# Softmax sums of two heads in one column-tiled block, values of both heads in the next iteration: a 32-head attention loop on one core

## The chip, the cores and the metric

The kernel runs on one core of a Trainium2 chip. The metric is the device time of one execution in microseconds. A ratio below is the mean time of one kernel's fast runs over that of the kernel before in the same rounds, so not quite the ratio of the medians that stand beside it; below 1 is faster. Times of different rounds are compared through the kernel before, which ran in all of them.

## The reference

Four layers in turn, each added to its input: a spectral filter (A), a memory attention (B), A, B. The change concerns B alone (shortened; `...` marks cuts):

```python
# x: (1, 2048, 640) bf16; 64 segments of 32 rows, 8 memory rows before each; 32 heads of 128
for s in range(n_seg):
    h = jnp.concatenate([mem, xs], axis=1)
    q, k, v = (jnp.einsum('btd,dhe->bhte', h, W) for W in (Wq, Wk, Wv))
    scores = jnp.where(mask, jnp.einsum('bhqe,bhke->bhqk', q, k) * scale, -1e9)
    p = _softmax(scores, axis=-1)
    o = jnp.einsum('bhqk,bhke->bhqe', p, v)
    o = jnp.einsum('bhte,hed->btd', o, Wo)
    mem = o[:, :M, :]
    ...
```

The kernel takes all segments at once with a guess for the memory rows, checks the guess, and falls back to a general path if it is off.

## The kernel before

Iteration `h` of the head loop projects K, Q and V of head `h`, computes scores of head `h - 1` (Exp on ScalarE, mask product on VectorE, giving P), sums P of head `h - 1` over the keys, and multiplies P of head `h - 2` with V. The **sums** use a stationary operand of ones with 32 columns. Four of them run side by side in the array, one for each quarter of its columns, writing partitions 0, 32, 64 and 96:

```python
        def sums(h, P, ps_last):
            psl = pa.tile([128, 512], FP32, name="psl", tag="psl", bufs=1)
            jobs = []
            for i in range(max(len(r) for r in runs[:-1])):
                for g_ in range(NG - 1):
                    t, (_, lo, hi, off) = runs[g_][i]
                    b = lo - st.q0[g_] + (PRE if g_ else 0)
                    jobs.append((g_, psl[:, b:b + hi - lo], off, i == 0, i == len(runs[g_]) - 1))
            tail, (_, lo, hi, off) = runs[-1][0][1], runs[-1][1][1]
            top = ps_last[:, 512 - SW:512]
            for g_ in range(NG - 1):
                jobs.append((g_, top, off + SW * g_, True, g_ < NG - 2))
            jobs.append((NG - 2, top[:, SW - (tail[2] - tail[1]):SW], tail[3], False, True))
            for g_, dst, off, first_, last_ in jobs:
                nc.tensor.matmul(dst[32 * g_:32 * g_ + 32, :], lhsT=ones[:, 0:32], rhs=P[:, off:off + dst.shape[1]], start=first_, stop=last_,
                                 skip_group_check=True)
            v, nx = x_view(psl, PRE, GS), GS * SEG
            nc.scalar.copy(out=sums_sb[:, 0:nx].rearrange("p (r s j) -> p r s j", r=16, j=2), in_=byclass(v))
            nc.scalar.copy(out=sums_sb[:, nx:nx + GS], in_=v[:, :, SEG])
            nc.scalar.copy(out=sums_sb[0:32, NR - PRE:NR], in_=psl[0:32, 0:PRE])
            nc.scalar.copy(out=sums_sb[:, NR - PRE - SW:NR - PRE], in_=top)

        def sums_ln(h):
            nc.scalar.activation(out=Rs[h % 2], in_=sums_sb, func=ACTF.Ln, bias=g["floor"][:, 0:1])
            if h:
                nc.gpsimd.tensor_tensor(out=accS, in0=accS, in1=sums_sb, op=ALU.add)
            else:
                nc.gpsimd.tensor_copy(out=accS, in_=sums_sb)
            if 0 < h < H - 1:
                sums_acc(h - 1)

        def sums_acc(h):
            if h:
                nc.gpsimd.tensor_tensor(out=accR, in0=accR, in1=Rs[h % 2], op=ALU.add)
            else:
                nc.gpsimd.tensor_copy(out=accR, in_=Rs[0])

        def sums_back(h):
            R = Rs[h % 2]
            nc.scalar.activation(out=R, in_=R, func=ACTF.Exp, scale=-1.0)
            if h == H - 1:
                return
            Rd = g["dram"].tile([1, 4 * NR], FP32, name="Rd", tag="Rd", bufs=3)
            nc.sync.dma_start(out=Rd[0:1, :].rearrange("o (g n) -> (o g) n", g=4), in_=R[0:128:32, :])
            nc.sync.dma_start(out=Rbs2[h % 2], in_=Rd[0:1, :].to_broadcast([128, 4 * NR]))
```

The reciprocals are a row per quarter; they go to DRAM and come back as a broadcast to all partitions, for VectorE to multiply with when it evicts the value matmuls from PSUM. They are made on ScalarE as Ln of the sums and Exp of the negated Ln. A chain is a row of matmuls that add up in one PSUM bank, for a run of some 500 columns five of them. `merge` deals the dependent work out between the dense units, a projection chain or two each:

```python
        def merge(dense, dep):

            n = 0
            for i, f in enumerate(dense):
                f()
                while n * len(dense) < (i + 1) * len(dep):
                    dep[n]()
                    n += 1

# ... in the loop, for each h:
                dense, parts, groups = [], [], []
                if h < H:
                    def both(run):
                        return [lambda: (run(w, h, NG - 1), run(w, h, 0))] + [lambda g_=g_: run(w, h, g_) for g_ in range(1, NG - 1)]

                    dense += both(k_run)
                    dense += [lambda: q_m(w, h)] if h < 2 else both(q_run)
                    vt = [lambda t=t: v_tiles(w, h // 2, t) for t in range(0, NT, 2)]
                    dense += vt[5:] if h % 2 else vt[:5]
                post = [lambda: None] * 3
                if 1 <= h <= H:
                    P[h - 1] = Ps[(h - 1) % 2]
                    Rb[h - 1] = Rbs2[(h - 1) % 2]
                    parts = [lambda part=part: last_ps.update({h - 1: score_part(h - 1, P[h - 1], part)}) for part in st.parts]
                    post = [lambda: sums(h - 1, P[h - 1], last_ps[h - 1]), lambda: sums_ln(h - 1), lambda: sums_back(h - 1)]
                if h >= 2:
                    oT[h - 2] = oTs[h % 2]
                    groups = [lambda g_=g_: value_group(h - 2, P[h - 2], Rb[h - 2], oT[h - 2], g_) for g_ in range(NG)]
                if h < H:
                    g1 = groups + [lambda: None] * (NG - len(groups))
                    merge(dense, parts + [g1[0], post[0], g1[1], post[1], g1[2], post[2], g1[3], g1[4]])
# ... (cut: iterations 32 and 33, and the output projection)
```

TensorE's PSUM banks: three for projections, two for scores, two for value groups, one for the wide sums. All are in use.

## Time and profile before

| | before |
|---|---|
| time, median of the 4 runs beside the changed kernel | 1572.94 us (1571.74 to 1574.16) |
| span in the profile | 1569.8 us |
| busy: TensorE, VectorE, ScalarE | 98%, 50%, 52% |
| two heads of the loop (even and odd) | 32.40 us |
| column-tiled blocks of sums in the two B layers | 64, of 21 matmuls each |

How to read it: TensorE is the only engine without idle time in the loop, so a pair of heads lasts as long as TensorE's stream of instructions. A matmul's end in the profile is computed (the prediction names the page of the Trainium skill that says so). For what a matmul really takes one goes by its start and the start of the next. "Edge" or "excess" below means the distance between two starts less what the first streams, its columns at 2.4 per ns, the rate that the prediction reads from the trace. The prediction shows the lines.

### The profile page before, as it was taken

The page shows a single profiled execution, that of the slowest core. Times are in us where ns is not written, and L with a number is a line of the kernel's source. Part 1 is how long each engine was busy: PE and PEld are TensorE (multiplying, and loading weights), DVE is VectorE, ACT ScalarE, POOL GpSimd, SP SyncE. Part 2 cuts the span into 40 slices and gives each one's busy share as a digit, 9 for nine tenths or more (in the row PEclk, how much of TensorE's full clock was granted, in tenths as well). Part 3 has the DMA queues.
Part 4 walks back from the last instruction along what each step waited for, and adds up shares of the span by engine and source line. Part 5 has one row for each costly group of instructions (what it writes and reads, how often), then busy time and mean ns, then how long its engine had stood idle before and what let it go on. Part 6 is the DMA issues. An engine that isn't in the chain of part 4 may idle for free. (4 is left out here: it accounts for less than half of the span.)

```text
span 1569.8 us, 36492 instructions
## 1 busy us (share of the span) xinstructions
PE 1536.3 (98%) x14418; PEld 1072.5 (68%) x14419; DVE 787.4 (50%) x2198; ACT 818.5 (52%) x2485; POOL 228.5 (15%) x327
## 2 busy tenths in 40 slices
PE   7999999999999999999999999999999999999998
PEld 5676676666766666677766766666766666677776
DVE  7872555455555545533377535455555545553111
ACT  4484665666666566511126655666666566662000
POOL 3620111111111111100034101111111111110000
PEclk9999999999999999999999999999999999999999
DMA  4680545446454553636114515446454554537242
GB/s 171 210 302 12 151 134 138 137 121 178 123 151 123 136 163 106 218 98 178 51 49 148 189 54 136 138 122 177 124 150 123 136 163 131 143 98 229 68 125 67
DMA packets 159763, 214.78 MB, mean 137 GB/s; under 512 B 7136, under 2 KB 133096, under 8 KB 151648
## 3 DMA queue, kind: packets, MB, share of 16 engines
q1 hardware_dynamic: 159008, 210.08, 45.8%
q8 instruction: 114, 1.87, 0.5%
q0 software_dynamic: 576, 2.30, 0.4%
q14 instruction: 65, 0.53, 0.1%
HBM read 167.26 MB, written 45.10 MB: 135 GB/s over the span
## 5 line engine op out<-in xcount | busy, mean ns | idle before, releaser
L1086 PEld LDWEIGHTS <-bB_S 128*128 128x128 bf16 x3180 | 258.2, 97 | 174.3 <-issue 0.9
L1245 DVE TENSOR_TENSOR bB_S<-pso,bB_S 128x480 bf16<-128x480 f32 (+1 forms) x320 | 194.2, 607 | 237.3 <-PE pso L1231 226.5
L1165 ACT ACTIVATE bB_S<-pss 128x269 bf16<-128x269 f32 (+5 forms) x576 | 204.2, 387 | 196.4 <-PE pss L1162 191.3
L1399 PE MATMUL psx<-Wo_sb,bB_S 128*128 128x320 bf16 x2048 | 287.7, 299 | 0.1
L1145 DVE CAST bB_S<-psk 128x495 bf16<-128x495 f32 (+3 forms) x320 | 191.7, 600 | 112.6 <-PE psk L1086 82.8
L1399 PEld LDWEIGHTS <-bB_S 128*128 128x128 bf16 x2048 | 197.1, 98 | 74.4 <-DVE bB_S L1245 0.7
L1166 DVE TENSOR_TENSOR bB_S<-bB_S,maskf 128x269 bf16<-128x269 bf16 (+5 forms) x576 | 158.3, 289 | 162.0 <-ACT bB_S L1165 162.0
L1154 ACT CAST bB_S<-psv 128x512 bf16<-128x512 f32 (+1 forms) x288 | 161.4, 560 | 86.5 <-PE psv L1152 83.3
L1130 ACT ACTIVATE bB_S<-psq 128x96 bf16<-128x96 f32 x300 | 152.7, 509 | 91.6 <-PE psq L1086 90.7
L1196 POOL TENSOR_TENSOR bB_S<-bB_S,bB_S 128x535 f32<-128x535 f32 x62 | 69.9, 1128 | 726.8 <-ACT bB_S L1191 713.9
L1152 PE MATMUL psv<-bB_S,B1hT_S 128*128 128x256 bf16 x1360 | 166.2, 273 | 0.0
L1152 PE MATMUL psv<-bB_S,B2hT_S 128*128 128x256 bf16 x1360 | 166.2, 273 | 0.0
L1086 PE MATMUL psk<-B1hT_S,bB_S 128*128 128x495 bf16 (+3 forms) x800 | 162.3, 343 | 0.3 <-ACT bB_S L1107 0.2
L1086 PE MATMUL psk<-B2hT_S,bB_S 128*128 128x495 bf16 (+3 forms) x800 | 162.3, 343 | 0.2 <-ACT bB_S L1107 0.2
L1162 PEld LDWEIGHTS <-bB_S 128*128 128x128 bf16 x1152 | 98.4, 98 | 84.4
L1086 PE MATMUL psq<-B1hT_S,bB_S 128*128 128x495 bf16 (+5 forms) x780 | 153.2, 336 | 0.0
L1086 PE MATMUL psq<-B2hT_S,bB_S 128*128 128x495 bf16 (+5 forms) x780 | 153.2, 336 | 0.0
L1152 PEld LDWEIGHTS <-B2hT_S 128*128 128x128 bf16 x1360 | 127.5, 98 | 13.3 <-issue 0.2
L1152 PEld LDWEIGHTS <-B1hT_S 128*128 128x128 bf16 x1360 | 127.5, 98 | 13.3 <-issue 0.2
L1162 PE MATMUL pss<-bB_S 128*128 128x132 bf16 (+8 forms) x1152 | 132.0, 219 | 0.1
L1231 PE MATMUL pso<-bB_S,bB_S 128*128 128x132 bf16 (+8 forms) x1152 | 118.9, 219 | 1.7 <-DVE oTmf L1248 1.2
L1231 PEld LDWEIGHTS <-bB_S 128*128 128x128 bf16 x1152 | 89.4, 98 | 20.5 <-DVE oTmf L1246 2.2
(281 smaller groups left out, 1472.8 us busy)
## 6 DMA issues: line engine op xcount, KB each, us to landing
bB_S<-Rd SPq DMA_DIRECT2D x62, 1070.0 KB
oTx_d<-bB_S SPq DMA_DIRECT2D x60, 512.0 KB
bB_S<-oTx_d SPq DMA_DIRECT2D x46, 512.0 KB
bB_S<-in_B_Wq_dram SPq DMA_DIRECT2D x32, 320.0 KB
bB_S<-in_B_Wk_dram SPq DMA_DIRECT2D x32, 320.0 KB
bB_S<-in_B_Wv_dram SPq DMA_DIRECT2D x32, 320.0 KB
Wo_sb<-in_B_Wo_dram SPq DMA_DIRECT2D x4, 1280.0 KB
B1wv_S<-in_B_Wv_dram SPq DMA_DIRECT2D x10, 512.0 KB
```

The lines of the kernel that those rows point to most:

```text
L1086: nc.tensor.matmul(ps, lhsT=w[:, ch, hh * 128:(hh + 1) * 128], rhs=src[:, ch, lo:hi], start=(ch == 0), stop=(ch == 4))
L1130: nc.scalar.mul(out=qv[:, :, 0:SEG], in_=x_view(ps, o, n)[:, :, 1:SW], mul=scale)
L1145: nc.vector.tensor_copy(out=KTs[h % 2][:, lo:hi], in_=ps[:, 0:hi - lo])
L1152: nc.tensor.matmul(ps[:, i * 256:(i + 1) * 256], lhsT=hT[:, ch, st.hcol((t + i) * 128):st.hcol((t + i) * 128) + 128], rhs=w["Wv"][:, ch, : ...
L1154: nc.scalar.copy(out=V[:, t:t + n, :].rearrange("p a b -> p (a b)"), in_=ps[:, 0:n * 256])
L1162: nc.tensor.matmul(ps[:, off - o0:off - o0 + hi - lo], lhsT=KT[:, t * 128:(t + 1) * 128], rhs=QT[:, lo:hi], start=True, stop=True)
L1165: nc.scalar.activation(out=E[:, 0:n], in_=ps[:, 0:n], func=ACTF.Exp)
L1166: nc.vector.tensor_tensor(out=P[:, o0:o0 + n], in0=E[:, 0:n], in1=bs.mask[:, o0:o0 + n], op=ALU.mult)
L1196: nc.gpsimd.tensor_tensor(out=accS, in0=accS, in1=sums_sb, op=ALU.add)
L1231: nc.tensor.matmul(pso[:, lo - q0:hi - q0], lhsT=V[:, t, (h % 2) * 128:(h % 2 + 1) * 128], rhs=P[:, off:off + hi - lo], start=(i == 0), st ...
L1245: nc.vector.tensor_tensor(out=oT.rearrange("p (r s j) -> p r s j", r=16, j=2)[:, :, s0:s0 + ns, :], in0=byclass(po), in1=rx, op=ALU.mult)
L1399: self.tc.nc.tensor.matmul(ps[:, 0:320], lhsT=lhs(h, k // 2), rhs=self.g["Wo_sb"][:, h, c0:c0 + 320], start=(h == 0), stop=(h == H - 1))
```

## The change

Its intent is to halve how often TensorE goes into the column-tiled mode and out of it. In even iterations one block holds the sums of two heads; the value matmuls of both wait for the following odd iteration, because only then are the reciprocals there. For pairs the copies of the sums from PSUM move from ScalarE to VectorE. The core of the diff:

```diff
-        def sums(h, P, ps_last):
-            psl = pa.tile([128, 512], FP32, name="psl", tag="psl", bufs=1)
-            jobs = []
-            for i in range(max(len(r) for r in runs[:-1])):
+        def sums(heads, ps_last):
+            jobs, outs = [], []
+            for n, h in enumerate(heads):
+                psl = pa.tile([128, 512], FP32, name="psl", tag="pso" if n else "psl", bufs=2 if n else 1)
+                top = ps_last[:, 512 - SW * (n + 1):512 - SW * n]
+                outs.append((sums_sb[h % 2], psl, top))
+                for i in range(max(len(r) for r in runs[:-1])):
+                    for g_ in range(NG - 1):
+                        t, (_, lo, hi, off) = runs[g_][i]
+                        b = lo - st.q0[g_] + (PRE if g_ else 0)
+                        jobs.append((h, g_, psl[:, b:b + hi - lo], off, i == 0, i == len(runs[g_]) - 1))
+            tail, (_, lo, hi, off) = runs[-1][0][1], runs[-1][1][1]
+            for n, h in enumerate(heads):
+                top = outs[n][2]
                 for g_ in range(NG - 1):
-                    t, (_, lo, hi, off) = runs[g_][i]
-                    b = lo - st.q0[g_] + (PRE if g_ else 0)
-                    jobs.append((g_, psl[:, b:b + hi - lo], off, i == 0, i == len(runs[g_]) - 1))
-            tail, (_, lo, hi, off) = runs[-1][0][1], runs[-1][1][1]
-            top = ps_last[:, 512 - SW:512]
-            for g_ in range(NG - 1):
-                jobs.append((g_, top, off + SW * g_, True, g_ < NG - 2))
-            jobs.append((NG - 2, top[:, SW - (tail[2] - tail[1]):SW], tail[3], False, True))
-            for g_, dst, off, first_, last_ in jobs:
-                nc.tensor.matmul(dst[32 * g_:32 * g_ + 32, :], lhsT=ones[:, 0:32], rhs=P[:, off:off + dst.shape[1]], start=first_, stop=last_,
+                    jobs.append((h, g_, top[:, :], off + SW * g_, n == 0, g_ < NG - 2))
+                jobs.append((h, NG - 2, top[:, SW - (tail[2] - tail[1]):SW], tail[3], False, True))
+            for h, g_, dst, off, first_, last_ in jobs:
+                nc.tensor.matmul(dst[32 * g_:32 * g_ + 32, :], lhsT=ones[:, 0:32], rhs=P[h][:, off:off + dst.shape[1]], start=first_, stop=last_,
                                  skip_group_check=True)
-            v, nx = x_view(psl, PRE, GS), GS * SEG
-            nc.scalar.copy(out=sums_sb[:, 0:nx].rearrange("p (r s j) -> p r s j", r=16, j=2), in_=byclass(v))
-            nc.scalar.copy(out=sums_sb[:, nx:nx + GS], in_=v[:, :, SEG])
-            nc.scalar.copy(out=sums_sb[0:32, NR - PRE:NR], in_=psl[0:32, 0:PRE])
-            nc.scalar.copy(out=sums_sb[:, NR - PRE - SW:NR - PRE], in_=top)
+            copy = nc.vector.tensor_copy if len(heads) == 2 else nc.scalar.copy
+            for sb, psl, top in outs:
+                v, nx = x_view(psl, PRE, GS), GS * SEG
+                copy(out=sb[:, 0:nx].rearrange("p (r s j) -> p r s j", r=16, j=2), in_=byclass(v))
+                copy(out=sb[:, nx:nx + GS], in_=v[:, :, SEG])
+                copy(out=sb[0:32, NR - PRE:NR], in_=psl[0:32, 0:PRE])
+                copy(out=sb[:, NR - PRE - SW:NR - PRE], in_=top)
 ...
-            Rd = g["dram"].tile([1, 4 * NR], FP32, name="Rd", tag="Rd", bufs=3)
-            nc.sync.dma_start(out=Rd[0:1, :].rearrange("o (g n) -> (o g) n", g=4), in_=R[0:128:32, :])
-            nc.sync.dma_start(out=Rbs2[h % 2], in_=Rd[0:1, :].to_broadcast([128, 4 * NR]))
+            Rd[h] = g["dram"].tile([1, 4 * NR], FP32, name="Rd", tag="Rd", bufs=4)
+            nc.sync.dma_start(out=Rd[h][0:1, :].rearrange("o (g n) -> (o g) n", g=4), in_=R[0:128:32, :])
+            if h % 2 or h == H - 2:
+                for a in range(h if h == H - 2 else h - 1, h + 1):
+                    nc.sync.dma_start(out=Rbs2[a % 2], in_=Rd[a][0:1, :].to_broadcast([128, 4 * NR]))
 ...
-                dense, parts, groups = [], [], []
+                dense, parts = [], []
                 if h < H:
                     def both(run):
                         return [lambda: (run(w, h, NG - 1), run(w, h, 0))] + [lambda g_=g_: run(w, h, g_) for g_ in range(1, NG - 1)]
 
-                    dense += both(k_run)
-                    dense += [lambda: q_m(w, h)] if h < 2 else both(q_run)
+                    ks, qs = both(k_run), [lambda: q_m(w, h)] if h < 2 else both(q_run)
                     vt = [lambda t=t: v_tiles(w, h // 2, t) for t in range(0, NT, 2)]
-                    dense += vt[5:] if h % 2 else vt[:5]
-                post = [lambda: None] * 3
+                    vt = vt[5:] if h % 2 else vt[:5]
+                    for n in range(5):
+                        dense += (ks[n:n + 1] if h % 2 else []) + qs[n:n + 1] + vt[n:n + 1]
+                    if h % 2 == 0:
+                        dense = ks + dense
+                pause = lambda: None
                 if 1 <= h <= H:
                     P[h - 1] = Ps[(h - 1) % 2]
                     Rb[h - 1] = Rbs2[(h - 1) % 2]
                     parts = [lambda part=part: last_ps.update({h - 1: score_part(h - 1, P[h - 1], part)}) for part in st.parts]
-                    post = [lambda: sums(h - 1, P[h - 1], last_ps[h - 1]), lambda: sums_ln(h - 1), lambda: sums_back(h - 1)]
-                if h >= 2:
-                    oT[h - 2] = oTs[h % 2]
-                    groups = [lambda g_=g_: value_group(h - 2, P[h - 2], Rb[h - 2], oT[h - 2], g_) for g_ in range(NG)]
+
+                def values(a):
+                    oT[a] = oTs[a % 2]
+                    return [lambda g_=g_: value_group(a, P[a], Rb[a], oT[a], g_) for g_ in range(NG)]
+
+                def post_of(*heads):
+                    return [lambda: sums(heads, last_ps[heads[-1]])] + [f for a in heads for f in (lambda a=a: sums_ln(a), lambda a=a: sums_back(a))]
+
                 if h < H:
-                    g1 = groups + [lambda: None] * (NG - len(groups))
-                    merge(dense, parts + [g1[0], post[0], g1[1], post[1], g1[2], post[2], g1[3], g1[4]])
+                    if h % 2 == 0:
+                        dep = parts + ([pause] + post_of(h - 2, h - 1) + [pause] * 11 if h else [])
+                    elif h == 1:
+                        dep = parts
+                    else:
+                        v0, v1 = values(h - 3), values(h - 2)
+                        v0[4] = lambda f=v0[4]: (f(), store(h - 3, oT[h - 3]))
+                        v1[4] = lambda f=v1[4]: (f(), store(h - 2, oT[h - 2]))
+                        if h < H - 1:
+                            dep = [pause, pause, v0[0]]
+                            for f, p in zip(v0[1:] + v1, parts):
+                                dep += [p, f]
+                        else:
+                            dep = [pause]
+                            for f, p in zip(v0, parts):
+                                dep += [f, p]
+                            dep += parts[5:] + [pause]
+                            for f, p in zip(post_of(h - 1), v1):
+                                dep += [f, p]
+                            dep += v1[3:]
```

Cut: two buffers for the sums in place of one, the accumulators for the range check, and iterations 32 and 33, which do the same as before.

## The prediction

> **What bounds the kernel now.** I read the page first, its busy row and its chain, then the chain of waits, then windows and the timeline inside the head loop of layer B, and last the timeline of the DMA queue. The page gives
>
> ```profile
> PE 1536.3 (98%) x14418; PEld 1072.5 (68%) x14419; DVE 787.4 (50%) x2198; ACT 818.5 (52%) x2485; POOL 228.5 (15%) x327
> PE 43%; DMA 0%; DVE 0%; ACT 0%; SPq 0%; issue 0%; DVEq 0%
> ```
>
> TensorE is busy for 98% of the span, VectorE and ScalarE for half of it, and of the chain that ended last every step that carries a share is TensorE's. Two heads of the loop, cut at the first K matmul of each, in windows:
>
> ```profile
> 430.36:462.75 32.39, 32.39 (x302) 21.96 (x301) 16.98 (x50) 20.41 (x65) 4.50 (x5) 1.00 0.47 132
> 445.74:462.75 17.01, 17.01 (x160) 11.71 (x159) 8.78 (x27) 10.40 (x33) 2.58 (x3) 1.00 0.56 155
> 462.75:478.14 15.39, 15.39 (x146) 10.26 (x145) 8.20 (x24) 10.02 (x32) 1.93 (x3) 1.00 0.37 107
> ```
>
> The columns are window, its length, busy us of PE, PEld, DVE, ACT and POOL, granted clock, DMA share and rate. The even head takes 17.01 us, the odd one 15.39 (it has four value-projection units where the even has five), PE without a gap in both, at the full clock. So a pair costs 32.40 us, and only TensorE's own instruction stream can shorten it; work that goes from ScalarE to VectorE buys nothing here by itself.
>
> A busy PE may still lose time between matmuls. I took the start of every matmul in the trace and subtracted from the distance to the next one the streaming time of the first, columns divided by 2.4 per ns (five matmuls of 499 columns start 1.05 us apart in all, below, which is that rate and 2 to 3 ns each). For the dense matmuls between 200 and 690 us the rest is 2 to 3 ns. It is large in two places only, at the two edges of the column-tiled softmax sums:
>
> ```profile
> 449.66 1.22 PE L1086 MATMUL psk<-B1hT_S,bB_S 128*128 128x499 bf16 x5
> 450.71 0.40 PE L1162 MATMUL pss<-bB_S 128*128 128x132 bf16 x4
> ...
> 439.58 1.22 PE L1086 MATMUL psq<-B1hT_S,bB_S 128*128 128x499 bf16 x5
> 440.73 0.42 PE L1185 MATMUL psl<-bB_S,ones 128*32 128x139 bf16 x16
> 440.98 0.20 PE L1185 MATMUL pss<-bB_S,ones 128*32 128x33 bf16 x5
> 441.12 0.41 PE L1231 MATMUL pso<-bB_S,bB_S 128*128 128x132 bf16 x4
> ```
>
> These are timeline rows: start, time, engine and line, tiles, count. Before an ordinary matmul the chain of five takes 450.71 - 449.66 = 1.05 us; before the block it takes 440.73 - 439.58 = 1.15 us, so **going in costs 0.10 us**. The block's 16 wide sums start over 0.25 us, 16 ns apart, a quarter of what one of some 132 columns streams (55 ns), so four column groups do run at once. The five narrow ones (33 or 5 columns) have 0.14 us to the next ordinary matmul, though they need some 0.05, so **coming out costs 0.09 us**. Over the 27 blocks between 200 and 690 us the medians are 97 ns in and 96 ns out; with the usual 3 ns taken off, 94 + 93 = 0.187 us a block. The chain of waits also holds
>
> ```profile
> PEld L1185 <- issue: 25.4, 62, 0.4
> ```
>
> which is not 0.41 us lost per block: it is the weight loader's idle time, most of it beside the matmuls of the Q chain. Only matmul starts count.
>
> **What the Trainium skill says.** "TensorEngine Tiling (Array Packing)", Key Properties, says that changing the tiling mode, unlike changing the tile, drains TensorE. It gives no figure; the trace agrees and gives 0.187 us for both ways. "TensorE: Matmul & The Clock Gate", section Back-to-back issue gap, has columns / 2.4 + 2.5 ns for a warm matmul; the trace has 2 to 3 ns over the streaming time. "Perfetto Trace Analysis", section Tensor Engine Instruction, says that a matmul's end in the profile is computed, not observed; hence I count from starts, and the 98% alone proves nothing.
>
> **The change part by part.**
> 1. *Fewer blocks.* In the built order of instructions I counted runs of 32-column matmuls: 64 runs of 21 before; after, 30 of 42 (one per pair, heads 0 to 29 of each of the two layers) and 4 of 21 (heads 30 and 31). The sum is 1344 both times, and TensorE has as many instructions as before. Thirty switches in and out go: 30 x 0.187 = **5.6 us**. Inside a block nothing changes; four groups are fed in the same rotation, and 42 take twice what 21 do.
> 2. *Sum copies go from ScalarE to VectorE* for pairs: 4 x 60 instructions. On ScalarE they take 0.58 + 0.22 + 0.17 + 0.21 = 1.18 us a head; VectorE's eviction of the same 480 columns takes 0.66, so some 1.2 us. ScalarE loses about 71 us in all, VectorE gains about 72. Neither is on the path: 0.
> 3. *Value matmuls of two heads in odd iterations.* TensorE's total is the same. From the pieces (K and Q 4.5 us each, a head's scores 1.0, its values 1.0, value projection 5.5 even and 3.8 odd, sums 0.3 a head) I estimate for the even iteration 4.5 + 4.5 + 5.5 + 1.0 + 0.6 + 0.2 = 16.3 us, and for the odd 4.5 + 4.5 + 3.8 + 1.0 + 2.0 = 15.8. VectorE in the odd one has five K casts of 0.60 (3.0 us), nine mask products of 0.29 (2.6) and the value evictions of two heads (5 x 0.61, and six small ones of 0.16: 4.0 a head): some 13.6 us of duration in 15.8, 86%. Consecutive VectorE rows overlap by about 0.1 us in the timeline, so the real load is lower. Busy, not the bound: 0.
> 4. *Broadcast of the reciprocals.* Today a write of the row and a broadcast per head, each iteration; after, both writes, then both broadcasts. No bytes more, but two broadcasts stand one behind the other. See the second rival.
> 5. *Ends.* Heads 30 and 31 and the output projection keep their order; the chain after the loop is unmoved: 0.
>
> Sum: 1574.06 - 5.6 = **1568.5 us**. A pair would take 32.40 - 0.19 = 32.21 us.
>
> **The rivals.**
> *A: VectorE or ScalarE holds PSUM back.* VectorE is strictly in order, and in the odd iteration value evictions, mask products (which wait for ScalarE's Exp) and K casts queue behind each other. Value groups come about 0.9 per projection unit, so two banks for them cover some 3 us, and an eviction ends some 2 us after its matmuls when a mask product ahead of it is late. The projection's three banks cover three units, also some 3 us. In the even iteration Ln, Exp, Ln, Exp (0.74 and 0.66) stand between Q and V evictions, and the first Ln waits for VectorE's copies; ScalarE should run about 1.5 us late for three units, still inside three banks. For it: both margins are about 1 us. Against it: PE waits for almost nothing in the loop today. If it comes, I would expect 0.2 to 0.5 us a pair, 6 to 15 us in all: 1569 to 1578.
>
> *B: the broadcast lands late.* Today:
>
> ```profile
> 461.61 0.50 SPq L1214 DMA_DIRECT2D Rd<-R  x1
> 463.36 0.34 SPq L1215 DMA_DIRECT2D bB_S<-Rd  x1
> ...
> 464.00:467.00 3.00, 3.00 (x23) 1.68 (x21) 2.27 (x6) 1.22 (x4) 0.00 (x0) 1.00 0.82 137
> 467.00:471.00 4.00, 4.00 (x30) 2.28 (x29) 2.21 (x7) 2.69 (x12) 0.00 (x0) 1.00 0.80 302
> ```
>
> The broadcast leaves 1.75 us after the row's write and moves 1.07 MB at 137 GB/s, later 302: 0.41 MB by 467 us, the rest 2.2 us later, so it lands about 5.9 us after its issue (estimate). Afterwards, from the end of the sums: copies and Ln to 1.9 us, second Exp at about 4.6, first broadcast issued at 5.2, landed at about 11.1. The first value group's matmuls end at about 10.4 (seven units of 1.05 to 1.1 in the even iteration, two of 1.3 in the odd one). VectorE would wait 0.7 us, and PE needs that bank again only at about 13.1. So I expect the wait to show on VectorE and to cost nothing; if the pair's two broadcasts slow each other by 2 us or more, PE stalls and up to 1 us a pair returns, 1569 to 1595 at worst. The second broadcast, needed some 7 us later, has room.
>
> *C: the idle time of the weight loader was a real loss of 0.41 us.* Then 30 x 0.41 = 12.3 us go, to about 1562. The starts of the matmuls speak against it.
>
> **Range and chances.** The gain has a ceiling near 5.6 us, since nothing else in the loop waits; the three runs of before spread over 2.3 us. Stalls of A or B might eat part or a little more than all. I take 1565.5 to 1574.5. A gain of 2% would need 31 us, over five times the switches removed: 0.01. A loss of 2% needs a stall of 1 us in every pair: 0.01. Within 2%: 0.98.
>
> **What would show it.** Right: 34 blocks, about 0.10 us into and 0.09 out of each, a pair period of 32.2 us, VectorE busy near 860 us and ScalarE near 748, no PE row in the chain of waits worth over a few us. B: an idle row of VectorE's value eviction released by the broadcast, and gaps at the third value group. A: gaps before value or projection matmuls in odd iterations, released by VectorE or ScalarE. The prediction is wrong if the pair period stays at 32.4 with the blocks halved, or falls well below 32.1, which would mean that a switch costs more than its edges show.

## The result, and the profile after

| | before | after |
|---|---|---|
| median, 4 runs each, same rounds | 1572.94 us | 1566.86 us (1565.62 to 1568.15) |
| ratio, 95% interval | | 0.9961, 0.9944 to 0.9979 |
| span in the profile | 1569.8 us | 1563.9 us |
| pair of heads | 32.40 us | 32.20 us |

The change is worth 6.1 us of the median, and 5.5 us in a second set of rounds (1572.76 less 1567.27, below): within 2%, but clear of the noise. The page after, its busy row and the chain that ended last:

```profile
PE 1529.1 (98%) x14418; PEld 1072.3 (69%) x14419; DVE 816.3 (52%) x2438; ACT 768.7 (49%) x2245; POOL 238.6 (15%) x329
PE 41%; DMA 1%; ACT 0%; DVE 0%; issue 0%; SPq 0%; DVEq 0%; ACTq 0%
```

TensorE has the same number of instructions, 14418 matmuls, and is 7.2 us less busy; ScalarE has 240 instructions fewer and VectorE 240 more, the 4 x 60 copies. In the windows of a pair, cut at the first K matmul of each head (columns as in the prediction):

```profile
443.12:475.32 32.20, 32.20 (x302) 22.01 (x301) 17.93 (x59) 18.75 (x58) 4.87 (x4) 1.00 0.39 134
443.12:459.39 16.27, 16.27 (x163) 10.99 (x162) 7.41 (x27) 10.73 (x32) 4.87 (x4) 1.00 0.41 118
459.39:475.32 15.93, 15.93 (x141) 11.01 (x139) 10.53 (x32) 8.01 (x26) 0.00 (x0) 1.00 0.37 150
```

Both halves are still full of TensorE work, and the pair is 0.20 us shorter than the 32.40 of before. VectorE now has 10.53 us in the odd half, ScalarE 10.73 in the even. The block itself, in TensorE's timeline (start, us, engine and line, tiles, count):

```profile
450.00 1.25 PE L1153 MATMUL psv<-bB_S,B1hT_S 128*128 128x256 bf16 x10
451.18 0.67 PE L1190 MATMUL psl<-bB_S,ones 128*32 128x139 bf16 x32
451.67 0.26 PE L1190 MATMUL pss<-bB_S,ones 128*32 128x33 bf16 x10
451.86 1.22 PE L1087 MATMUL psq<-B1hT_S,bB_S 128*128 128x495 bf16 x5
```

From the V chain's first matmul to the block are 1.18 us, where its ten matmuls need 10 x (256 / 2.4 + 2.5 ns) = 1.09; the edge in is there once, and once more on the way out. Over all blocks of the trace, one of 42 lasts 0.769 us with both edges, one of 21 lasted 0.481. Two of 21 against one of 42 is 2 x 0.481 - 0.769 = 0.193 us of the 0.20 that a pair gains. Of the rows that are new in the list of waits, this one bears on rival B:

```profile
DVE bB_S L1250 <- DMA bB_S<-Rd: 57.6, 31, 4.7
```

VectorE's value evictions wait for the broadcast of the reciprocals, 1.8 us a pair on average ((57.6 - 4.7) / 30; the wait of 4.7 us stands at the end of the second layer). Before, they had waited for TensorE in all but 2 of 237 us. That wait and what it costs are the subject of one experiment.

### The profile page after: what moved, and what is told of

It reads as the page before. It is cut to its first block, busy times and chain, and to the rows that moved or that the text cites. A ratio compares the mean times of both kernels' runs of the same rounds, so it can differ in the third digit from the quotient of the medians.

```text
span 1563.9 us, 36413 instructions
## 1 busy us (share of the span) xinstructions
PE 1529.1 (98%) x14418; PEld 1072.3 (69%) x14419; DVE 816.3 (52%) x2438; ACT 768.7 (49%) x2245; POOL 238.6 (15%) x329
## 5 line engine op out<-in xcount | busy, mean ns | idle before, releaser
L1166 ACT ACTIVATE bB_S<-pss 128x269 bf16<-128x269 f32 (+5 forms) x576 | 208.9, 386 | 138.6 <-PE pss L1163 138.3
L1206 POOL TENSOR_TENSOR bB_S<-bB_S,bB_S 128x535 f32<-128x535 f32 x90 | 111.6, 1253 | 820.0 <-DVE bB_S L1198 762.2
L1250 DVE TENSOR_TENSOR bB_S<-pso,bB_S 128x480 bf16<-128x480 f32 (+1 forms) x320 | 192.6, 602 | 75.1 <-DMA bB_S<-Rd 57.6
L1163 PE MATMUL pss<-bB_S 128*128 128x132 bf16 (+8 forms) x1152 | 137.6, 219 | 0.0
```

Source lines behind the costliest of these rows:

```text
L1163: nc.tensor.matmul(ps[:, off - o0:off - o0 + hi - lo], lhsT=KT[:, t * 128:(t + 1) * 128], rhs=QT[:, lo:hi], start=True, stop=True)
L1166: nc.scalar.activation(out=E[:, 0:n], in_=ps[:, 0:n], func=ACTF.Exp)
L1206: nc.gpsimd.tensor_tensor(out=acc, in0=acc, in1=part, op=ALU.add)
L1250: nc.vector.tensor_tensor(out=oT.rearrange("p (r s j) -> p r s j", r=16, j=2)[:, :, s0:s0 + ns, :], in0=byclass(po), in1=rx, op=ALU.mult)
```

## The experiments

The theory: **what is saved is the way into and out of the column-tiled mode, 0.19 us each time**. Rivals: the new order of values and projections, or ScalarE's relief, made the gain; or an extra weight load is what costs. All kernels gave correct results.

### Sums of the two heads in two blocks again

Everything else of the change stays. The first attempt:

```diff
-dep = parts + ([pause] + post_of(h - 2, h - 1) + [pause] * 11 if h else [])
+dep = parts + ([lambda: sums((h - 2,), last_ps[h - 1], 0, True),
+               lambda: sums((h - 1,), last_ps[h - 1], 1, True)]
+              + post_of(h - 2, h - 1)[1:] + [pause] * 11 if h else [])
```

with `sums` taking the place `n` of a lone head, and copies on VectorE.

> The changed kernel, but the two heads' softmax sums stand in two column-tiled blocks of 21 matmuls with one projection unit between them, in place of one block of 42; value matmuls, copies on VectorE, order of Ln, Exp and broadcasts stay. Theory (the gain is the switching in and out of the column-tiled mode): 64 blocks again, a pair period of 32.20 + 0.19 = 32.39 us, the whole about 30 x 0.19 = 5.7 us slower than the changed kernel, so equal to the kernel before within 1 us (ratio 0.999 to 1.001). Rival (the gain is from the new order of value matmuls and of the projections, or from ScalarE's relief): the pair period stays at 32.20 and the time at about 1567 us.

Measured: 1594.25 us, ratio 1.0138 (1.0121 to 1.0154), a pair of 33.15 us. That fits neither theory. The chain of waits, TensorE's rows, names what happened:

```profile
PE pss L1190 <- ACT bB_S L1166: 16.9, 30, 0.6
```

The narrow sums (into pss) of the first block use the bank of the last scores. In this edit they follow those scores without a projection unit between them, and TensorE waits for ScalarE's Exp to have read the bank: 30 times, with an excess of 0.73 us between the matmul starts. The edit had brought in a wait of its own. Less that wait the pair would be 33.15 - 0.73 = 32.42 us, near the 32.39 of the theory, but that is a subtraction and no test. Mended: the lone first block puts its narrow sums into a value bank, which is idle in even iterations.

```diff
 top = ps_last[:, 512 - SW * (n + 1):512 - SW * n]
+if alone and n == 0:
+    top = pa.tile([128, 512], FP32, name="pso", tag="pso")[:, 0:SW]
 ...
-jobs.append((h, g_, top[:, :], off + SW * g_, n == 0, g_ < NG - 2))
+jobs.append((h, g_, top[:, :], off + SW * g_, n == 0 or alone, g_ < NG - 2))
```

> The split into two blocks of 21 again, mended. In the first split run the pair period was 33.15 us, of which 0.73 us was one wait that the edit itself had brought in: the narrow sums of the first block go into the bank of the last scores and now followed them directly, so they waited for ScalarE's Exp of those scores. Here the first block's narrow sums go into a bank that is idle in even iterations, and nothing else differs from the first split. Theory (switches): no such wait, 64 blocks, period 32.39 us, 5.7 us over the changed kernel, ratio to before 0.999 to 1.001. Rival (order of values or ScalarE's relief): 32.20 us and 1567 us.

Measured: 1573.43 us against 1573.41 for the kernel before, ratio 1.000 (0.9984 to 1.0017). A pair in windows:

```profile
349.06:381.46 32.40, 32.40 (x302) 22.01 (x301) 18.06 (x59) 18.75 (x58) 4.86 (x4) 1.00 0.44 149
```

With two blocks in place of one the whole gain is gone, though values still come in pairs, the projections keep their new order and the copies stay on VectorE. This rules out the order and ScalarE's relief. It also answers what the pairing of the values is for: by itself it gives nothing, it only makes room for the common block.

### A lone matmul with 32, 128 and 96 stationary columns

Two matmuls a pair are added in even iterations, apart from each other, into the sums' bank, for nobody to read (here with 32):

```diff
+def extra():
+    ps = pa.tile([128, 512], FP32, name="psl", tag="psl", bufs=1)
+    nc.tensor.matmul(ps[0:32, 0:132], lhsT=ones[:, 0:32], rhs=P[h - 1][:, 0:132], start=True, stop=True, ...)
-dep = parts + ([pause] + post_of(h - 2, h - 1) + [pause] * 11 if h else [])
+dep = parts + ([pause] + post_of(h - 2, h - 1) + [pause] * 2 + [extra] + [pause] * 3 + [extra] + [pause] * 4 if h else [])
```

> The changed kernel plus two lone matmuls a pair, each of 32 stationary columns and 132 streamed ones, apart from each other and from the sums, into a bank whose result nobody reads; output unchanged. Theory: each is a block of its own and pays 0.055 us of streaming and 0.19 us of switching, so 0.48 us a pair: period 32.68 us, 30 x 0.48 = 14.5 us slower than the changed kernel, about 1581 us. Rival (an extra matmul costs only its streaming, the edges seen in starts are made up elsewhere): 0.11 us a pair, about 3.5 us in all.

> As the run with two lone matmuls of 32 stationary columns, but with 128 stationary columns, so without a change of mode. Theory: 0.058 us each, 0.12 us a pair: period 32.32 us, 3.5 us slower than the changed kernel, about 1570.5 us. Rival (any lone matmul with other weights between two chains costs as much): 0.48 us a pair, about 1581 us.

> As the run with two lone matmuls of 128 stationary columns, but with 96, which is [...]not a full weight load. Theory (the cost is the drain at a change of mode): as with 128 columns, period 32.32 us, about 1570.5 us. Rival (the cost is a slower weight load that is not hidden when fewer than 128 columns are loaded): edges of 50 to 190 ns at each, period 32.4 to 32.7 us, 1573 to 1581 us.

| stationary columns | time, median | ratio to before (95%) | pair | edge in, out (medians of 60) |
|---|---|---|---|---|
| 32 | 1581.93 us | 1.0058 (1.0041 to 1.0074) | 32.73 us | 97, 109 ns |
| 128 | 1570.76 us | 0.9991 (0.9974 to 1.0007) | 32.31 us | 4, 4 ns |
| 96 | 1570.98 us | 0.9989 (0.9972 to 1.0006) | 32.31 us | 4, 4 ns |

All three came out as the theory had it, within 1 us. The same lone matmul between a chain of 499 or 495 columns and a V chain, with 32, 128 and 96 stationary columns, in TensorE's timeline of each kernel:

```profile
460.62 1.22 PE L1087 MATMUL psq<-B1hT_S,bB_S 128*128 128x499 bf16 x5
461.77 0.23 PE L1328 MATMUL psl<-bB_S,ones 128*32 128x132 bf16 x1
461.93 2.36 PE L1153 MATMUL psv<-bB_S,B1hT_S 128*128 128x256 bf16 x20
```

```profile
487.77 1.21 PE L1087 MATMUL psq<-B1hT_S,bB_S 128*128 128x495 bf16 x5
488.82 0.22 PE L1328 MATMUL psl<-bB_S,ones 128*128 128x132 bf16 x1
488.88 1.25 PE L1153 MATMUL psv<-bB_S,B1hT_S 128*128 128x256 bf16 x10
```

```profile
325.84 1.21 PE L1087 MATMUL psq<-B1hT_S,bB_S 128*128 128x495 bf16 x5
326.90 0.22 PE L1328 MATMUL psl<-bB_S,ones 128*96 128x132 bf16 x1
326.95 1.25 PE L1153 MATMUL psv<-bB_S,B1hT_S 128*128 128x256 bf16 x10
```

The starts tell it: 461.77 - 460.62 = 1.15 us to the narrow one and 0.16 from it to the next; 1.05 and 0.06 us with 128, 1.06 and 0.05 with 96, where the chain of five alone needs 1.04 and the lone matmul 0.06. The rows' own durations (0.23 and 0.22 us) hardly differ and would have told nothing. With 32 columns each addition costs (32.73 - 32.20) / 2 = 0.27 us a time for 0.055 us of streaming, with 128 or 96 columns 0.057 us. So the edges are real time, and they come with the 32-column matmuls alone: 96 columns cost no more than 128. No run had 64.

The weight loads of these lone matmuls, from `--source L1328` of the three kernels (duration in ns, least, median and most, then first and last start):

```profile
L1328 PEld LDWEIGHTS <-ones x60: 92/92/93, 164.8 to 1402.4; 128*32 128x32 bf16 x60
L1328 PEld LDWEIGHTS <-ones x60: 98/98/98, 165.5 to 1390.7; 128*128 128x128 bf16 x60
L1328 PEld LDWEIGHTS <-ones x60: 124/124/124, 165.1 to 1391.0; 128*96 128x96 bf16 x60
```

The load of 96 columns does take longer, 124 ns against 98, but it starts 0.21 us before its matmul, as that of 128 does, so the longer load stays hidden: the rival of the short weight load falls. The load of 32 columns starts 1 or 2 ns before its matmul, 60 times of 60, and the first load of each block of sums does so too (0 to 3 ns in the changed kernel); on the way out the lead is 4 ns in the median. At a switch, then, no weight load runs ahead. What remains open is why: whether the array drains, as the page that the prediction cites has it, or the weight load is held back until the old mode is over. That neither a load nor a matmul starts within an edge (95 to 97 ns in and out of a block) before its last 5 ns fits the first, that an edge is about as long as a weight load (92 to 98 ns) the second; no run separates them.

### The copies back on ScalarE

```diff
-copy = nc.vector.tensor_copy if len(heads) == 2 else nc.scalar.copy
+copy = nc.scalar.copy
```

> The changed kernel with the pair's eight sum copies back on ScalarE. In the trace of the changed kernel VectorE's copies let the first Ln start 0.86 us after the last of the sums' matmuls; on ScalarE eight copies take 1.5 us of starts behind the V eviction, so the first Ln should start 0.5 us later, the second Exp and the broadcasts too. The first value eviction then ends 0.5 us later; the third value group's matmul has 0.8 us of slack there, so no stall from it. ScalarE's evictions of Q and V lag 0.5 us more, where the projection's banks have about 0.5 us left. Theory of the prediction (where the copies run is worth nothing by itself): period 32.20 to 32.25 us, 0 to 1.5 us over the changed kernel. Rival (moving the copies is part of the gain): period at or above 32.3 us, 3 to 9 us over it.

Measured: 1567.24 us, ratio 0.9963 (0.9946 to 0.998), a pair of 32.20 us. Counted from the block's first matmul, the first Ln starts after 1.89 us (1.54 in the changed kernel) and the broadcasts are issued after 5.93 us (5.60), medians of 30: 0.3 us later, less than the 0.5 expected, and TensorE does not notice. Moving the copies is no part of the gain, nor was it needed for it.

### The block one projection unit later

```diff
-dep = parts + ([pause] + post_of(h - 2, h - 1) + [pause] * 11 if h else [])
+dep = parts + ([pause] * 3 + post_of(h - 2, h - 1) + [pause] * 9 if h else [])
```

> The changed kernel with the sums block and all that follows it (Ln, Exp, broadcasts) one projection unit, 1.05 us, later. In the trace of the changed kernel VectorE waits 1.7 us for the first broadcast and its eviction is over at 464.15 us, 0.8 us before TensorE starts the third value group in that bank. Theory (the broadcast is hidden with 0.8 us of slack and not more): the eviction ends 1.05 us later, TensorE stalls 0.2 to 0.4 us a pair, period 32.4 to 32.6 us, 6 to 12 us over the changed kernel; VectorE's wait for the broadcast about 2.8 us a pair. Rival (the wait on VectorE is absorbed further, or the broadcast isn't what frees it): period 32.20 us. Blocks and edges unchanged in both.

Measured: 1580.30 us, ratio 1.0046 (1.0029 to 1.0063), a pair of 32.58 us in the median (32.35 to 32.87). First and third value group in the changed kernel, VectorE's eviction and TensorE's matmuls in the same bank:

```profile
463.34 0.66 DVE L1250 TENSOR_TENSOR bB_S<-pso,bB_S 128x480 bf16<-128x480 f32 x1 [1.72 <-DMA bB_S<-Rd]
...
463.99 0.16 DVE L1253 TENSOR_TENSOR oTmf<-pso,bB_S 128x7 bf16<-128x7 f32 x1
...
464.95 0.40 PE L1236 MATMUL pso<-bB_S,bB_S 128*128 128x132 bf16 x4
```

and with the later block:

```profile
468.73 0.66 DVE L1250 TENSOR_TENSOR bB_S<-pso,bB_S 128x480 bf16<-128x480 f32 x1 [2.88 <-DMA bB_S<-Rd]
...
469.38 0.16 DVE L1253 TENSOR_TENSOR oTmf<-pso,bB_S 128x7 bf16<-128x7 f32 x1
...
469.60 0.41 PE L1236 MATMUL pso<-bB_S,bB_S 128*128 128x132 bf16 x4 [0.25 <-DVE oTmf L1253]
```

In the brackets are the engine's idle time and what ended it. In the changed kernel the bank is free at 463.99 + 0.16 = 464.15 us and TensorE comes for it 0.8 us later. With everything 1.05 us later VectorE waits 2.88 us, and TensorE now waits for VectorE: the sum of these excesses between starts is 10.0 us over 28 pairs, and in the last odd iterations, where the first value group comes early, 2.9 us in place of 0.8. Together 12 of the 13 us. So the wait in the changed kernel's profile is free, with 0.8 us to spare, and a change that lengthens the way of the reciprocals by 1 us costs twice what the change gained.

### The ends of the loops

The trace of the changed kernel has new stalls of TensorE in the last odd iteration of each layer, 0.46 and 0.34 us, and after the loop it keeps old ones where value groups of head 30 stand three in a row. The first attempt delays the values in the last odd iteration and deals out the value groups between output matmuls:

```diff
-dep = [pause]                 # iteration 31
+dep = [pause] * 3
 ...
 for i, f in enumerate(wide):  # iteration 32
     f()
-    for _ in range(2):
-        (fill or groups).pop(0)()
+    fill.pop(0)()
+    (fill if i < 2 else groups).pop(0)()
```

> An attempt at a better kernel, at the end of each layer's loop alone: in the last odd iteration the first value group comes one unit later, as in the others (the trace of the changed kernel has a stall of 0.46 us there in one layer and 0.34 in the other), and in the output part after the loop the value groups of head 30 alternate with output matmuls in place of standing three in a row (stalls of 0.75 and 0.40 us a layer). Theory: about 1.4 us a layer goes, 2 to 3 us in all, so about 1564 us, pair period 32.20 as before. Rival (the stalls move to the next place, because the broadcast of head 30 or the copies decide): within 0.5 us of the changed kernel.

Measured: 1565.83 us, ratio 0.995 (0.9934 to 0.9967). In its trace, from first K to last value matmul, the two loops are 520.35 and 520.41 us against 521.19 and 521.25. That is 0.84 us a layer where 1.4 were expected. The stalls named are gone or smaller; a new one of 0.52 us a layer is there, where four score parts stand in a row with two banks, so a part of them moved on, as the rival had it. Three more kernels ran together to compare in the same rounds:

> The changed kernel unaltered, five rounds beside the kernel before and the two attempts below, to compare all on one chip. Theory: 1567 us, ratio 0.995 to 0.997. If it came out within 0.1% of the kernel before, the gain of the first measurement would be a matter of the chip.

> The first attempt at the layers' ends again, unaltered, five rounds. Its trace had the two loops 1.7 us shorter than the changed kernel's, its time 1565.8 us in other rounds. Theory: 1 to 2.5 us under the changed kernel of the same rounds. Rival (difference of rounds): within 0.5 us of it.

> The first attempt's new stall mended: there four score parts stood in a row in the last odd iteration, with two banks, and TensorE waited 0.52 us a layer for ScalarE's Exp. Here a value group stands between the second and the third of them and the sums of head 30 come one unit later. Theory: that stall goes, 0.5 us a layer, so 1 us under the first attempt and 2 to 3.5 us under the changed kernel, about 1564.5 us. Rival (the broadcast of head 30, now one unit later, becomes the wait at its value groups): no better than the first attempt.

| five runs each, same rounds | median | all | ratio to before |
|---|---|---|---|
| changed kernel | 1567.27 us | 1566.27 to 1568.55 | 0.9969 (0.9956 to 0.9983) |
| first attempt at the ends | 1565.52 us | 1565.08 to 1565.62 | 0.9956 (0.9942 to 0.997) |
| second attempt | 1566.59 us | 1566.24 to 1567.23 | 0.9964 (0.9951 to 0.9978) |

The changed kernel repeats its gain (0.9969, inside the 0.995 to 0.997 expected). The first attempt beats both kernels: its slowest run is faster than the changed kernel's fastest, by little, and by 1.75 us in the median. The intervals of the ratios overlap, so this rests on the runs of these rounds and on the loops' lengths. In this run's trace, though, only the first layer's loop was shorter (520.33 against 521.12 us; 521.50 against 521.08 in the second, where one stall of 1 us between an output and a value matmul stood that the first run's trace didn't have), so where all of the 1.75 us lies is not settled. The second attempt was no better. Its sums of head 30 come later, their Ln and Exp now stand in front of the first scores of head 31 on ScalarE, and TensorE waits for it, as in this line of its timeline:

```profile
639.14 0.28 PE L1163 MATMUL pss<-bB_S 128*128 128x132 bf16 x2 [0.34 <-ACT bB_S L1166]
```

So the rival's kind of outcome, a wait that moves on, but at ScalarE and not at the broadcast that it named.

## Why the prediction was right

*TensorE's stream is the bound.* It held: a pair lasts exactly as long as TensorE is busy in it, before and after, and taking work from ScalarE or giving it back moved nothing.

*Thirty switches at 0.187 us, 5.6 us.* It held, in count (34 blocks) and size. (In the trace of before 28 blocks, not 27, start between 200 and 690 us; the medians are as the prediction has them.) By the lengths of the blocks it is 0.193 us a pair, 30 x 0.193 = 5.8 us; the sum of the excesses at all switches in the loops falls from 12.32 to 6.50 us, 5.8 as well. The loops are 2.83 and 2.70 us shorter, 5.53 of the 6.0 us by which the two spans differ. The rest lies outside the loops, in code that the change hardly touches, where the traces differ more than that from run to run: the loop's first K matmul starts at 132.9 to 135.2 us over all runs. So it is no sign of a larger price that the median shows 6.1 us and not 5.6; its interval, 0.9944 to 0.9979, is 3.3 to 8.8 us. The foretold 1568.5 us is 1.6 over the measured median because it starts from 1574.06, the median of three runs of before; from 1572.94, that of four, it would be 1567.3. That the switches are the cause, and not only accompany it, is shown by the split into two blocks (all of it lost) and by the lone matmuls (0.21 us of edges with 32 columns, 0.008 with 96 or 128).

*Periods.* Foretold were 32.21 us for a pair, 16.3 and 15.8 for its halves; measured 32.20, 16.27 and 15.93.

*Copies to VectorE are worth nothing by themselves.* Shown for the changed kernel by putting them back. The busy times foretold beside it were mis-sized: VectorE was to gain some 72 us and ScalarE to lose 71, but VectorE gained 28.9 and ScalarE lost 49.8. I had added durations, while busy time counts overlapping rows once: the 240 copies on VectorE have 67.0 us of durations, but cover 51.3 us. Putting the copies back moved VectorE from 816.3 to 764.6 us and ScalarE from 768.7 to 801.1, so the copies themselves are 51.7 and 32.4 us; the rest, -22.8 and -17.4, came with the new order. That more overlap made this rest is not tested.

*Rival A, PSUM held back by VectorE or ScalarE.* It did not come in the steady pairs: there is no excess over 30 ns between TensorE's starts there but at the switches.

*Rival B, the late broadcast.* As foretold, the wait shows on VectorE and costs TensorE nothing, but its size was off: 0.7 us expected, 1.72 in the pair shown. Most of this is the view: it counts VectorE's idle time from the end of its last K cast, while I had counted from the end of the value matmuls, at 462.49 us (462.08 + 0.41 in TensorE's timeline, a computed end), from where 463.34 is 0.85 us. In the measure of the prediction it is 0.85 against 0.7. The first broadcast is issued at 456.79 us, and VectorE's wait for it ends at 463.34, 6.6 us later (5.9 estimated). The slack at the third value group was 0.8 us, where the prediction's times leave about 1.2 (13.1 less 11.1 and 0.8 for the eviction). One unit more and it is a stall: rival B is real, and the kernel is 1 us away from it.

*Rival C, 0.41 us for each block.* It fell: 0.19 us a block, and 0.27 us for a lone tiled matmul with its streaming. In the changed kernel the loader's idle time before a block is 6.7 us in 32 waits, 0.21 each in place of 0.41, while the edges stay at 95 and 96 ns: it is no measure of the price. By estimate it is two matmuls of the chain before the block, of 499 columns in the kernel before (2 x 0.21 us) and of 256 in the changed one (2 x 0.11).

*Ends worth nothing.* Right to 0.6 us, not in the detail. Stalls of 0.95 us at the first heads of the two layers went (0.24, 0.28, 0.24 and 0.19 us, where scores and K chains had waited), and 0.80 us came in the last odd iterations, where the first value group stands one unit earlier than in the others; between value matmuls of the last heads 2.45 us of waits became 3.15.

## What to carry to other kernels

Where TensorE is the bound, as here, count how often its tiling mode changes and gather the tiled matmuls into fewer, longer blocks; measure the price by the starts of matmuls, since durations and the busy share hide it. Pairing iterations to do so delays what hangs on the tiled results, so check how much slack the longest way back has, here a write, a broadcast and an eviction with 0.8 us to spare. And when an experiment undoes a part of a change, look first whether the edit has put two users of one bank next to each other.

## What the Trainium skill lacked or had wrong

- "TensorEngine Tiling (Array Packing)", section Key Properties, says that a change of tiling mode drains TensorE and gives no price. Here it is 97 ns in and 96 ns out for a block of 21 matmuls, 95 and 96 for the changed kernel's, in a stream of dense bf16 matmuls at full clock, and 97 and 109 ns for a block of one. Nor does it say what a single matmul of a width in between costs among full ones: with 96 stationary columns the edges are 4 ns in and 4 ns out, as with 128.
- "TensorE: Matmul & The Clock Gate", section Weight-path perf modes, has the fast weight load on only when all 128 columns are loaded. It doesn't say when its loss shows: single loads of 96 columns in a dense stream took 124 ns against 98, and cost nothing, since they start 0.21 us ahead (32.31 us a pair, as with 128).
- The same page, section Step-by-step: what each phase is for, has TensorE pull weight loads ahead of running matmuls, where row groups don't conflict or the load goes to the background buffer. It doesn't say that this stops at a change of mode: the first load of each of the 64 blocks of the kernel before starts 1 or 2 ns before its matmul and the first one after it 4 or 5 ns, against 210 ns for a lone matmul of 128 columns.
